# Attention beside the direct blocks of an FFN kernel: three engines in source order, five places per tile, one mixing matmul per tile of the next batch

## The chip, the core and the metric

The kernel runs on one core of one Trainium2 chip. The metric is the time of one execution on the device, in microseconds (us). A core has TensorE (PE; its weight loads are shown apart as PEld), VectorE (DVE), ScalarE (ACT), GpSimd (POOL) and SyncE (SP), which issues nearly all transfers here. Each engine works off a queue of its own in order and waits on semaphores. TensorE's clock is granted at one of two levels, 1.2 or 2.4 GHz; the profile gives the granted clock as a share of the higher one.

## The reference, cut to what matters

Three stages: attention against pooled keys and values, a mixer over tokens with a feed-forward network (FFN), and a Fourier mixer with a normalised FFN.

```python
# 1. B, H, S, D = 8, 8, 576, 64; keys and values are means over 8 positions
k_p = k.reshape(B, H, 72, 8, D).mean(axis=3); v_p = v.reshape(B, H, 72, 8, D).mean(axis=3)
scores = q @ k_p.T / 8; scores -= scores.max(-1)
attn = exp(scores); x = attn / (attn.sum(-1) + 1e-9) @ v_p          # -> (B, S, 512)
# 2. token mixing of rank 32, then FFN 512 -> 2048 -> 512
u = x + ((x.transpose(0, 2, 1) @ U) @ V).transpose(0, 2, 1)
x1 = u + np.maximum(u @ w_ch1, 0) @ w_ch2
# 3. 2D Fourier transform, real part, layer norm, FFN 512 -> 2048 -> 512
u2 = x1 + np.real(fft(fft(x1, axis=1), axis=2)); un = layernorm(u2)
out = u2 + np.maximum(un @ w2_ch1, 0) @ w2_ch2
```

## The kernel before

Everything is fp32 accuracy on TensorE: a matrix is split into a high half (fp32r) and the rest, and a product is three matmuls. `split` (line 108) is that: a ScalarE copy for the high half and a VectorE subtraction for the low one. The 4608 token rows are worked in blocks. First comes a setup (to some 70 us): batch 0's attention, its mixing, the first columns.

**Direct blocks** are the stage that the change is about (some 70 to 862 us): six groups `gi` of 512 rows, and in each group 16 *slots* `f`, one for each 128 hidden columns. A slot has a first product `st1` (line 972: twelve matmuls into bank h0, then `hh` by ScalarE on line 988 and `hl` by VectorE on line 989) and, one slot late, a second product `st2` in two halves (line 995: twelve matmuls in all into four banks of sums). At a group's end the sums are added to their rows and stored (`finish`, line 1015).

Beside that run *lanes*, Python generators, of which the loop on lines 1179 to 1228 takes a step at a time; a yield ends a step, and what a step emits stands in the source between the matmuls of the slot. A slot has two *places* (i = 0, 1), one for each half of `st2`:

- `a` (lines 1054 to 1065), the attention of batches 1 to 7, five tiles of 128 rows each. In `tile_steps` (line 460) a tile takes three steps: scores into banks s0 and s1, with the maximum on VectorE and eight exponentials on ScalarE; the turn of the exponentials through s0 and s1 with two ScalarE copies; the products with V into s0, the scaling on VectorE, the split (`xh`, `xl`) and a store to `xd`. The rank-32 matmuls `hu_mm` of a tile (bank hu) come in the next tile's first step. In group 0 the lane takes a step in each place, later in three of four.
- `mix` (lines 1071 to 1076): when a batch's five tiles are done (`mix_split`, line 545), one matmul for each tile in bank s1 and a VectorE add to the row tile loaded back from `xd` (`mix_mm`, line 552), then a store to `ud`. One tile a place, five in consecutive places. When all five are done, `state["u"]`, the number of rows of `ud` that are ready, moves on.
- `prep`: the pooling of the next batch's keys and values on VectorE; `w`: conversion of weights from 64-bit words (`w_first` for the direct blocks; from group 1 on `w_combine` and `w_second` for the later stages); `p`: the next group's rows loaded, turned (`turn`, VectorE) and split (`settle`) into columns `utx`; `d`: the Fourier stage, once all lanes but `p` are done (`spectral`).

`until` (line 1098) steps lanes without block matmuls until a condition holds. It stands at two points: `p` is started once the next group's rows are in `ud`, from slot 11 on (slot 15 in group 0) by waiting for them; and after slot 15 `until` runs `p` to its end, outside the last group by stepping all lanes. The last splits of the next group's columns follow it.

What sets the order: a planner orders each engine's instructions by its own estimate of times. `manual_schedule` keeps the source's order for the engines that it names: ScalarE from group 1 on (line 1181), and TensorE and VectorE too in the last stage (`chain`, line 1269). `later` and `clock` delay a store to the next slot's start in the source. After 862 us comes the **Strassen stage**: the remaining direct rows and all of the second FFN with seven instead of eight products, with the Fourier lane beside it.

Of the kernel before, what the change touches and what calls it, by code (L numbers as in the profile page):

```python
# [8 lines left out]
F32 = mybir.dt.float32  # L9
F32R = mybir.dt.float32r  # L10
# [11 lines left out]
NPAIR = H // 2  # L22
# [20 lines left out]
NU = 5  # L43
F64_BIAS = float.fromhex("0x1p-112")
# [3 lines left out]
def kernel(  # L48
# [282 lines left out]
    class Attn:  # L331
        def __init__(self, c):
# [12 lines left out]
            self.mixing = False  # L345
            self.done = {}
            self.xq = [scratch(12 + t) for t in range(5)]
# [187 lines left out]
        def tiles(self, b):  # L535
            prev = None
            for t in range(5):
                yield from self.tile_steps(b, t, 0, prev)
                prev = (lambda t=t, x=self.done.pop(t): self.hu_mm(b, t, *x))
            prev()  # L540
            while self.mixing:
                yield
            self.mix_split(b)

        def mix_split(self, b):
            self.mixing = True
# [5 lines left out]
        def mix_mm(self, b, t, x):  # L552
# [5 lines left out]
            if t == 4:  # L558
                self.mixing = False

        def mix(self, b):
            xl = {}

            def load(t):
                n = TT[t][1]
                xl[t] = self.xtile(b)
                nc.sync.dma_start(out=xl[t][:n], in_=xd[b][t])
            load(0)
            yield
            load(1)  # L570
            yield
            for t in range(5):
                self.mix_mm(b, t, xl.pop(t))
                yield
                if t + 2 < 5:
                    load(t + 2)
# [247 lines left out]
    def pair_prep(js):  # L824
        yield from turn(js[0])
        for t in range(NT):
            settle(js[0], t)
            yield
        yield from turn(js[1])
# [185 lines left out]
    def finish(js):  # L1015
        for t in range(4):
# [37 lines left out]
    def lane_a(at):  # L1054
        for b in range(1, B):
# [3 lines left out]
            yield  # L1059
# [9 lines left out]
    mixq = []  # L1069

    def lane_mix(at):
        for b in range(1, B):
            while not mixq:
                yield
            yield from at.mix(mixq.pop(0))
            state["u"] = (b + 1) * S
# [21 lines left out]
    def until(cond, names=None):  # L1098
        n = 0
        state["tick"] = 0  # L1100
        while not cond():
# [4 lines left out]
            assert n < 500, (state, list(lanes))  # L1106

# [33 lines left out]
    lanes["mix"] = lane_mix(at)  # L1141
# [291 lines left out]
```

## Time and profile before

| | us |
|---|---|
| three runs | 1968.53, 1973.78, 1976.72 |
| median | 1973.78 |
| the profiled execution | 1970.54 |
| its span, first to last instruction | 1968.7 |
| TensorE busy in the span | 1846.7 (94%) |
| TensorE weight loads busy | 1596.0 (81%) |
| VectorE, ScalarE, GpSimd busy | 1020.5, 703.7, 196.1 |
| mean granted clock of TensorE | 0.977 |

A busy time is the union of an engine's instructions. Matmuls are pipelined and their ends are modelled, so a busy TensorE is not TensorE at its peak. A wait names the engine and the tile that was waited for, with the line of the instruction that made it. Lines 103, 106 and 113 are helpers (`sub`, `add`, `mm`), so an instruction is told by its tile's name: `utx` the columns of a block, `wo`, `cv` and `wr` weights, `x` rows, `s`, `h`, `o`, `m`, `hu` the banks of PSUM.

### The profile page before, as it was taken

The page shows a single profiled execution, that of the slowest core. Times are in us where ns is not written, and L with a number is a line of the kernel's source. Part 1 is how long each engine was busy: PE and PEld are TensorE (multiplying, and loading weights), DVE is VectorE, ACT ScalarE, POOL GpSimd, SP SyncE. Part 2 cuts the span into 40 slices and gives each one's busy share as a digit, 9 for nine tenths or more (in the row PEclk, how much of TensorE's full clock was granted, in tenths as well). Part 3 has the DMA queues.
Part 4 walks back from the last instruction along what each step waited for, and adds up shares of the span by engine and source line. Part 5 has one row for each costly group of instructions (what it writes and reads, how often), then busy time and mean ns, then how long its engine had stood idle before and what let it go on. Part 6 is the DMA issues. An engine that isn't in the chain of part 4 may idle for free.

```text
span 1968.7 us, 29395 instructions
## 1 busy us (share of the span) xinstructions
PE 1846.7 (94%) x10424; PEld 1596.0 (81%) x10424; DVE 1020.5 (52%) x2265; ACT 703.7 (36%) x2072; POOL 196.1 (10%) x341
## 2 busy tenths in 40 slices
PE   5787689898989999999999999999999999999999
PEld 4676578687767787889899989899989999999998
DVE  7763455555564544444455665656565434444332
ACT  7752434343434341323332433333333323232321
POOL 3430022112121000000000000000000000000000
PEclk9898889899999999999999999999999999999999
DMA  9743463756564646165758786858586766757564
GB/s 360 248 143 112 123 195 133 206 166 206 176 199 152 185 135 202 32 230 196 260 183 287 234 284 194 264 193 263 186 267 192 232 192 210 230 181 234 182 214 129
DMA packets 265779, 394.26 MB, mean 200 GB/s; under 512 B 61664, under 2 KB 92480, under 8 KB 265632
## 3 DMA queue, kind: packets, MB, share of 16 engines
q1 hardware_dynamic: 264704, 388.97, 62.1%
q0 software_dynamic: 928, 3.40, 0.5%
q8 instruction: 83, 1.36, 0.3%
q14 instruction: 64, 0.52, 0.1%
HBM read 312.73 MB, written 79.56 MB: 199 GB/s over the span
## 4 chain that ended last, share of the span: by engine, by line
PE 62%; DMA 3%; DVE 2%; ACT 1%; issue 0%; SPq 0%; DVEq 0%; ACTq 0%
PE h L113 28%; PE o L113 15%; PE m L113 7%; PE hu L113 7%; PE s L113 4%; PE s L901 1%; DMA wr<-wc 1%; DMA x<-x 0%; DMA ul<-ud 0%; DMA ud<-x 0%; DMA x1d<-ur 0%; DMA R<-x1d 0%; DVE hl L1254 0%; DVE xl L103 0%; DVE side L106 0%
## 5 line engine op out<-in xcount | busy, mean ns | idle before, releaser
L113 PEld LDWEIGHTS h<-x,wr 128*128 128x128 f32 x4032 | 527.4, 191 | 31.2 <-DVE side L106 2.5
L113 PE MATMUL h<-x,wr 128*128 128x256 f32 x4032 | 547.6, 283 | 5.2 <-DMA wr<-wc 2.3
L113 PE MATMUL o<-w,hh 128*128 128x512 f32 x1152 | 324.5, 404 | 11.4 <-ACT hh L988 11.2
L113 PE MATMUL h<-utx,w 128*128 128x512 f32 (+1 forms) x1164 | 288.5, 397 | 12.5 <-DVE utx L103 5.7
L113 PEld LDWEIGHTS h<-utx,w 128*128 128x128 f32 x1164 | 219.5, 192 | 62.3 <-DVE utx L103 6.9
L113 PEld LDWEIGHTS o<-w,hh 128*128 128x128 f32 x1152 | 202.8, 192 | 50.0 <-ACT hh L988 21.3
L106 DVE TENSOR_TENSOR side<-h,side 128x256 f32<-128x256 f32 x192 | 106.1, 553 | 145.7 <-PE h L113 144.9
L113 PE MATMUL o<-w,hl 128*128 128x512 f32 x576 | 179.3, 391 | 0.0
L113 PE MATMUL m<-w,hh 128*128 128x512 f32 x576 | 165.5, 395 | 0.2 <-DVE ur L106 0.2
L1248 ACT ACTIVATE hh<-side 128x256 fp32r<-128x256 f32 x192 | 100.0, 521 | 118.5 <-DVE side L106 118.5
L1248 ACT ACTIVATE hh<-h 128x256 fp32r<-128x256 f32 x96 | 36.9, 384 | 278.3 <-PE h L113 275.9
L113 PEld LDWEIGHTS o<-w,hl 128*128 128x128 f32 x576 | 107.9, 188 | 23.6
L1254 DVE SCALAR_TENSOR_TENSOR hl<-h,hh 128x256 fp32r<-128x256 f32 x96 | 40.6, 423 | 157.5 <-ACT hh L1248 157.3
L1254 DVE SCALAR_TENSOR_TENSOR hl<-side,hh 128x256 fp32r<-128x256 f32 x192 | 105.7, 550 | 24.7 <-ACT hh L1248 24.7
L988 ACT ACTIVATE hh<-h 128x512 fp32r<-128x512 f32 x96 | 56.9, 593 | 170.5 <-PE h L113 170.3
L113 PEld LDWEIGHTS m<-w,hh 128*128 128x128 f32 x576 | 103.1, 191 | 17.7 <-DVE ur L106 0.7
L989 DVE SCALAR_TENSOR_TENSOR hl<-h,hh 128x512 fp32r<-128x512 f32 x96 | 65.8, 685 | 87.6 <-ACT hh L988 87.2
L488 ACT ACTIVATE s<-s,mx 128x72 f32<-128x72 f32 x296 | 91.3, 333 | 47.8 <-DVE mx L485 46.0
L113 PE MATMUL hu<-w,hh 128*128 128x512 f32 x384 | 104.7, 394 | 0.0
L113 PE MATMUL m<-w,hl 128*128 128x512 f32 x288 | 97.6, 393 | 0.0
L103 POOL TENSOR_TENSOR wo<-wo 128x256 fp32r<-128x256 f32 x88 | 69.5, 809 | 280.4 <-ACT wo L109 250.5
L103 DVE TENSOR_TENSOR x<-ul,x 128x256 fp32r<-128x256 f32 x154 | 59.2, 420 | 39.6 <-ACT x L109 39.4
(239 smaller groups left out, 2445.0 us busy)
## 6 DMA issues: line engine op xcount, KB each, us to landing
wr<-wc SPq DMA_DIRECT2D x336, 512.0 KB
wc<-wo SPq DMA_DIRECT2D x88, 256.0 KB
x<-x SPq DMA_DIRECT2D x56, 256.0 KB
ur<-ud SPq DMA_DIRECT2D x36, 256.0 KB
x1d<-ur SPq DMA_DIRECT2D x36, 256.0 KB
ul<-u2d SPq DMA_DIRECT2D x36, 256.0 KB
ur<-u2d SPq DMA_DIRECT2D x36, 256.0 KB
out<-ur SPq DMA_DIRECT2D x36, 256.0 KB
```

The source lines that it names most:

```text
L103: eng.tensor_tensor(out=o, in0=a, in1=b, op=ALU.subtract)
L106: eng.tensor_tensor(out=o, in0=a, in1=b, op=ALU.add)
L113: nc.tensor.matmul(o, a, b, start=start, stop=stop, skip_group_check=True)
L488: nc.scalar.activation(out=s[:n, a], in_=v[:, k], func=ACTF.Exp, bias=mx[:n, a:a + 1], accum_out=sm[:n, a:a + 1])
L901: nc.tensor.transpose(o[:, k * 128:k * 128 + 128], u[:, k * 128:k * 128 + 128], ident)
L988: nc.scalar.activation(out=hh, in_=o, func=ACTF.Relu)
L989: nc.vector.scalar_tensor_tensor(out=hl, in0=o, scalar=0.0, in1=hh.bitcast(F32), op0=ALU.max, op1=ALU.subtract)
L1248: nc.scalar.activation(out=hh[:, i], in_=c, func=ACTF.Relu)
L1254: nc.vector.scalar_tensor_tensor(out=hl[:, i], in0=c, scalar=0.0, in1=hh[:, i].bitcast(F32), op0=ALU.max, op1=ALU.subtract)
```

## The change

- `order` now names TensorE, ScalarE and VectorE, from group 1 to the end of the kernel; `chain` is dropped.
- A slot of the direct blocks has three places; the halves of `st2` stand in the first two. Lane `a` steps in all three, `d` in two, `w` four times a slot, `prep` once, `p` three times. In group 0 and once `a` has ended there are further steps of `w`, `prep` and `p`.
- A tile of attention takes five places: scores (and the `hu` matmuls of the tile before), nothing, the turn, the products with V, nothing. `tile_steps` stays for batch 0.
- Lane `mix` is dropped. From batch 3 on, the step with the products with V also mixes the same tile of the batch before, and then loads its next tile. Batches 1 and 7 are mixed by themselves behind their tiles, a tile every second place. `state["u"]` moves with every mixed tile.
- `pair_prep` starts in slot 1 of every group and waits by itself for the rows of each of its blocks. The points of `until` are slot 14 (rows) and slot 15 (end of `p`, stepping `p` alone), both ahead of `st1`; in the last group slot 9. The last splits and the loads of `finish` follow `st1` of slot 15 at once.
- `finish` adds two sums behind each half of the last `st2`.

```diff
+        def kq(self, b, t):
+            q = self.q.pop((b, t))
+            sc = bank("s0"), bank("s1")
+            for p in range(NPAIR):
+                mm(sc[p // 2][:, (p % 2) * 144:(p % 2) * 144 + 144], q[:, p], self.k[:, p], p % 2 == 0, True)
+            self.q_load(5 * b + t + QAHEAD)
...
+            for i in range(2):
+                v = sc[i][:, 0:288].rearrange("p (h k) -> p h k", h=4)
+                nc.vector.tensor_reduce(out=mx[:, 4 * i:4 * i + 4], in_=v, op=ALU.max, axis=AX.X, negate=True)
+                for k in range(4):
+                    a = 4 * i + k
+                    nc.scalar.activation(out=s[:, a], in_=v[:, k], func=ACTF.Exp, bias=mx[:, a:a + 1], accum_out=sm[:, a:a + 1])
...
+        def exp_turn(self):
+            e0, e1 = bank("s0"), bank("s1")
+            for c in range(4):
+                nc.tensor.transpose(e0[:, c * 128:c * 128 + 128], self.s[:, c * 128:c * 128 + 128], ident)
+            nc.tensor.transpose(e1[:, 0:128], self.s[:, 512:640], ident)
...
+            nc.scalar.activation(out=e[:, 0:512], in_=e0, func=ACTF.Copy)
+            nc.scalar.activation(out=e[:, 512:640], in_=e1[:, 0:128], func=ACTF.Copy)
...
+        def av(self, b, t):
+            o = bank("s0")
...
+            xf = self.xtile(b)
+            nc.vector.tensor_tensor(out=xf.rearrange("p (h d) -> p h d", h=H), in0=o.rearrange("p (h d) -> p h d", h=H),
+                                    in1=self.cur.unsqueeze(2).to_broadcast([128, H, D]), op=ALU.mult)
...
+            split(xh, xl, xf)
+            store(xd[b][t], xf[:TT[t][1]])
+            self.done[t] = xh, xl
...
+        def mix_load(self, b, t):
+            n = TT[t][1]
+            self.xm[t] = self.xtile(b)
+            nc.sync.dma_start(out=self.xm[t][:n], in_=xd[b][t])
+
+        def mix_one(self, b, t):
+            self.mix_mm(b, t, self.xm.pop(t))
+            later(lambda: state.update(u=b * S + TT[t][0] + TT[t][1]))
...
     def pair_prep(js):
-        yield from turn(js[0])
-        for t in range(NT):
-            settle(js[0], t)
-            yield
-        yield from turn(js[1])
+        for j in js:
+            while state["u"] < (j + 1) * T:
+                yield
+            yield from turn(j)
+            if j == js[0]:
+                for t in range(NT):
+                    settle(j, t)
+                    yield
...
             at.kv_k(b)
-            yield
             at.kv_v(b)
             started.add(b)
             yield
-            yield from at.tiles(b)
-            mixq.append(b)
-            yield
+            beside = b > 2
+            if beside:
+                at.mix_load(b - 1, 0)
+            for t in range(5):
+                at.kq(b, t)
+                if t:
+                    at.hu_mm(b, t - 1, *at.done.pop(t - 1))
+                yield
+                yield
+                at.exp_turn()
+                yield
+                at.av(b, t)
+                if beside:
+                    at.mix_one(b - 1, t)
+                    if t < 4:
+                        at.mix_load(b - 1, t + 1)
+                yield
+                yield
+            at.hu_mm(b, 4, *at.done.pop(4))
+            at.mix_split(b)
+            yield
+            if b in (1, B - 1):
...
         if gi == 1:
-            order.enter_context(tc.manual_schedule(engines={mybir.EngineType.Activation}))
+            order.enter_context(tc.manual_schedule(engines={mybir.EngineType.PE, mybir.EngineType.Activation, mybir.EngineType.DVE}))
...
+            if last:
+                if f == 9:
+                    until(lambda: state["u"] >= (SB + 1) * TA)
+                if f == 6:
+                    lanes["p"] = prep_a(0)
+            else:
+                if f == 1:
+                    lanes["p"] = pair_prep(groups[gi + 1])
+                if f == NF - 2:
+                    until(lambda: state["u"] >= (gi + 2) * TA)
+                if f == NF - 1:
+                    until(lambda: "p" not in lanes, ["p"])
             hs = st1(js, f, gi == f == 0)
...
+            if f == NF - 1:
+                if not last:
+                    for t in range(NT):
+                        settle(groups[gi + 1][1], t)
+                for t in range(4):
+                    rest(js, t)
...
-            for i in range(2):
-                slot += 1
-                if gi == 0 or slot % 4:
-                    step("a")
-                step("d")
-                if prev:
+            for i in range(3):
+                step("a")
+                if i != 1:
+                    step("d")
+                if prev and i < 2:
                     st2(prev[1], prev[2], i)
-                for name in ("p", "mix", "w", "prep", "w") if f % 4 else ("p", "mix", "w", "prep"):
+                    if prev[1] == NF - 1:
+                        finish(prev[0], (2 * i, 2 * i + 1))
+                for name in (("w", "p"), ("prep", "w", "p"), ("w", "p", "w", "prep"))[i]:
                     step(name)
-                if last:
+                if last or gi == 0:
                     step("p")
-                    step("p")
+                if "a" not in lanes:
+                    step("w")
+                if gi == 0:
+                    step("prep")
+                    step("w")
```

## Rows read from the trace of the kernel before

**Rows 1.** The page, part 2: TensorE's granted clock in 40 slices, tenths.

```profile
PEclk9898889899999999999999999999999999999999
```

**Rows 2.** Windows by stage: stretch, length, busy time of each engine, clock, DMA.

```profile
181.00:247.00 66.00, 38.64 (x167) 28.17 (x166) 28.46 (x54) 23.88 (x102) 2.22 (x5) 0.78 0.51 138
247.00:372.00 125.00, 111.99 (x501) 89.74 (x500) 71.88 (x149) 45.23 (x169) 27.15 (x37) 0.94 0.58 178
372.00:508.00 136.00, 126.45 (x568) 101.14 (x567) 74.34 (x157) 54.51 (x203) 26.30 (x35) 0.94 0.62 185
508.00:641.00 133.00, 121.89 (x563) 98.26 (x562) 72.09 (x151) 53.88 (x200) 22.64 (x31) 0.96 0.56 176
641.00:759.00 118.00, 112.71 (x530) 91.73 (x530) 63.52 (x150) 43.47 (x149) 2.31 (x5) 1.00 0.51 153
759.00:862.00 103.00, 98.56 (x457) 79.85 (x456) 37.12 (x81) 21.10 (x47) 7.17 (x21) 1.00 0.40 126
862.00:1969.00 1107.00, 1095.14 (x6979) 990.81 (x6977) 555.76 (x1325) 353.84 (x885) 48.98 (x140) 1.00 0.68 220
```

**Rows 3.** TensorE's waits from 181 to 247: us in total, times, longest.

```profile
PE s L113 <- DVE x L106: 11.0, 5, 4.1
PE s L492 <- ACT s L488: 6.3, 4, 2.9
```

**Rows 4.** Windows of the six clusters in groups 1 to 3.

```profile
253.00:285.00 32.00, 25.65 (x112) 20.54 (x111) 21.96 (x44) 8.35 (x32) 5.32 (x7) 0.92 0.84 235
357.00:376.00 19.00, 13.34 (x44) 9.36 (x44) 12.97 (x25) 6.42 (x25) 0.00 (x0) 0.72 0.87 259
470.00:486.00 16.00, 12.98 (x50) 10.22 (x50) 8.53 (x17) 5.41 (x24) 2.15 (x3) 0.79 0.67 221
498.00:511.00 13.00, 9.81 (x35) 7.07 (x35) 9.66 (x22) 6.53 (x26) 1.79 (x2) 0.87 0.80 240
558.00:587.00 29.00, 23.83 (x99) 18.57 (x98) 18.04 (x38) 10.36 (x46) 3.61 (x5) 0.88 0.72 233
630.00:646.00 16.00, 12.14 (x49) 8.80 (x48) 9.46 (x23) 7.25 (x27) 0.00 (x0) 0.89 0.73 209
```

**Rows 5.** TensorE's waits from 320 to 870, for the next group's columns.

```profile
PE h L113 <- DVE utx L103: 5.7, 3, 2.5
...
PE h L113 <- ACT utx L109: 3.0, 3, 1.1
```

**Rows 6.** In order of time, 410 to 426: start, us, engine, line, operation, [idle before].

```profile
410.25 2.88 PE L113 MATMUL h<-utx,w 128*128 128x512 f32 x12
...
412.97 0.61 PE L113 MATMUL o<-w,hl 128*128 128x512 f32 x2
...
414.79 0.71 PE L113 MATMUL s<-k,q 128*128 128x144 f32 x4
...
417.53 0.32 ACT L488 ACTIVATE s<-s,mx 128x72 f32<-128x72 f32 x1 [0.70 <-DVE mx L485]
...
419.62 0.35 ACT L488 ACTIVATE s<-s,mx 128x72 f32<-128x72 f32 x1
...
425.11 2.88 PE L113 MATMUL h<-utx,w 128*128 128x512 f32 x12
```

**Rows 7.** Groups of instructions, 150 to 870: busy us, mean ns | idle before.

```profile
L103 POOL TENSOR_TENSOR wo<-wo 128x256 fp32r<-128x256 f32 x88 | 69.5, 809 | 280.4 <-ACT wo L109 250.5 <-DVE wo L103 14.0 <-DVE sm L498 8.5
...
L989 DVE SCALAR_TENSOR_TENSOR hl<-h,hh 128x512 fp32r<-128x512 f32 x85 | 58.2, 685 | 73.3 <-ACT hh L988 72.9
...
L152 DVE SCALAR_TENSOR_TENSOR wo<-cv,wo 128x256 int32<-128x256 int32 x32 | 16.0, 500 | 1.0
...
L152 DVE SCALAR_TENSOR_TENSOR cv<-wo,cv 128x256 int32<-128x256 int32 x32 | 13.3, 422 | 0.7
```

**Rows 8.** VectorE's waits from 320 to 870, for transfers.

```profile
DVE ul L809 <- DMA ul<-ud: 16.5, 10, 5.1
DVE cv L147 <- DMA wd<-cv: 14.5, 11, 2.0
```

More of the change, by code (lines that the diff above doesn't have):

```diff
@@ L43 @@
 NU = 5
+DEBUG = False
 F64_BIAS = float.fromhex("0x1p-112")
@@ L344, in __init__ @@
             self.raw = {}
-            self.mixing = False
             self.done = {}
+            self.xm = {}
             self.xq = [scratch(12 + t) for t in range(5)]
@@ L533, in first @@
                 yield
[L535 to L541, printed above, removed]
-                yield
-            self.mix_split(b)
+        def kq(self, b, t):
[4 more added lines that the diff above has]
+            self.q_load(5 * b + t + QAHEAD)
+            p1 = self.p
+            mx = p1.tile([128, H], F32, tag="mx", name="mx", bufs=2)
+            sm = p1.tile([128, H], F32, tag="sm", name="sm", bufs=2)
+            s = self.s[:, 0:S].rearrange("p (h k) -> p h k", h=H)
+            for i in range(2):
[4 more added lines that the diff above has]
+                    nc.scalar.activation(out=s[:, a], in_=v[:, k], func=ACTF.Exp, bias=mx[:, a:a + 1], accum_out=sm[:, a:a + 1])
+            self.cur = sm
@@ new lines, in exp_turn @@
+        def exp_turn(self):
[3 more added lines that the diff above has]
+            nc.tensor.transpose(e1[:, 0:128], self.s[:, 512:640], ident)
+            e = self.e = self.p.tile([128, 640], F32, tag="e", name="e")
+            nc.scalar.activation(out=e[:, 0:512], in_=e0, func=ACTF.Copy)
+            nc.scalar.activation(out=e[:, 512:640], in_=e1[:, 0:128], func=ACTF.Copy)
+            nc.vector.tensor_scalar(out=self.cur, in0=self.cur, scalar1=1e-9, scalar2=None, op0=ALU.add)
+            nc.vector.reciprocal(out=self.cur, in_=self.cur)
@@ L1013, in rest, with finish @@
         nc.sync.dma_start(out=res[t], in_=ud[r0:r0 + 128, :])
-    def finish(js):
-        for t in range(4):
+    def finish(js, ts=range(4)):
+        for t in ts:
             r = res.pop(t)
@@ L1058, in lane_a @@
             at.kv_k(b)
-            yield
             at.kv_v(b)
@@ L1062, in lane_a @@
             yield
-            yield from at.tiles(b)
-            mixq.append(b)
-            yield
+            beside = b > 2
[18 more added lines that the diff above has]
+            at.mix_split(b)
+            yield
+            if b in (1, B - 1):
+                at.mix_load(b, 0)
+                at.mix_load(b, 1)
+                yield
+                for t in range(5):
+                    yield
+                    at.mix_one(b, t)
+                    yield
+                    if t + 2 < 5:
+                        at.mix_load(b, t + 2)
     ready = set()
     started = {0}
[L1069 to L1076, printed above, removed]
     def lane_prep(at):
@@ L1106, in until @@
             assert n < 500, (state, list(lanes))
+        if n and DEBUG:
+            print("until", n, names, state["slot"], state["u"], list(lanes))
     lanes = {}
@@ L1191 @@
                 ring_load(f - NOP)
-            if not begun and f >= (6 if last else 2):
-                rows = (SB + 1) * TA if last else (gi + 2) * TA
-                ok = lambda: state["u"] >= rows
-                if f >= (NF - 1 if gi == 0 else 11):
-                    until(ok)
-                if ok():
-                    begun = True
-                    lanes["p"] = prep_a(0) if last else pair_prep(groups[gi + 1])
+            if f == NF - 1:
[4 more added lines that the diff above has]
+                    rest(js, t)
             if not df:
@@ L1267 @@
     prev, rows, low = None, None, None
-    chain = ExitStack()
-    chain.enter_context(tc.manual_schedule(engines={mybir.EngineType.PE, mybir.EngineType.DVE}))
     for k in range(len(seq)):
@@ L1327 @@
         st2_a(prev, t)
-    chain.close()
     order.close()
```

31 lines of the change are left out of this document (5 added, 26 removed).

## The prediction

> **What bounds the kernel now.** I read the page first, then the windows by stage, then TensorE's waits inside the bad windows, then one undisturbed stretch in order of time. In the page's forty slices the granted clock of TensorE is full almost everywhere; its dips lie in the first third [rows 1]. The windows tell why. From 862 us on (the Strassen stage) TensorE is busy 1095.14 of 1107 us at clock 1.00, so nothing is to be had there. The direct stage before it is not full. I put the loss of a window as its idle time plus (1 - clock) x length. From 181 to 247 that is 27.4 + 0.22 x 66 = 41.9 us; then 20.5, 17.7 and 16.4 us in the next three windows, 5.3 and 4.4 us in the last two: 106 us in 681 [rows 2]. This stage is bound by TensorE where TensorE has work at hand, and by the latency of the attention chain where it has not.
>
> The 106 us lie in few places.
> - The burst, 181 to 247. Counting places in the source, the last slot of group 0 runs `until` for 16 rounds: the mixing of batch 1 and nearly all attention of batch 2 are emitted with hardly a block matmul between them. TensorE then waits 11.0 us for the VectorE adds of the mixing (five times, all through bank s1), and for ScalarE's exponentials [rows 3]; the clock falls to 1.2 GHz after such idle stretches. 41.9 us.
> - Six clusters in groups 1 to 3, two a group. One is the mixing of five tiles in consecutive places, beside tiles of the next batch that want the same two banks (253, 470, 558 us); the other is the group's end, where the next group's last columns are split after the last block matmul at hand (357, 498, 630 us). By the same formula: 8.9, 11.0, 6.4, 4.9, 8.7 and 5.6 us, 45.5 us in all [rows 4]. At group ends TensorE waits 5.7 us for the VectorE half of the split and 3.0 us for the ScalarE half [rows 5].
> - The rest, 106 - 41.9 - 45.5 = 19 us, is spread over 681 - 66 - 125 = 490 us, about 4%.
>
> **The change part by part.** *Places.* A slot goes from two places to three, and the attention lane takes a step in each (before, three of four from group 1 on). A tile takes five places instead of three. Counted by hand, batch 1 ends its mixing in slot 13 of group 0 instead of behind slot 15, batch 2 starts in slot 14, and no `until` has to run the attention: what is left is two rounds of the p lane at the end of group 0 and none at the later ends. So the burst goes. Its tiles still cost TensorE their matmuls, now beside block matmuls.
>
> *What a place hides.* Twelve block matmuls take 412.97 - 410.25 = 2.72 us; a slot has 24, so 5.44 us, and half of the second product 1.36 us. Two slots with one tile take 425.11 - 410.25 = 14.86 us, which leaves 14.86 - 10.88 = 4.0 us per tile, small waits in it [rows 6]. Three places a slot at five a tile are 0.6 tiles a slot: 5.44 + 0.6 x 4.0 = 7.8 us, against 7.4 now at half a tile. From the scores to the turned exponentials there are two places. In the trace the first score matmul starts at 414.79, the first exponential at 417.53 and the last ends at 419.97: 2.4 us of exponentials, 5.2 us in all, but 417.53 was late because the second half of the scores waited for its bank and VectorE did `hl` in between [rows 6]. With `hl` (0.685 us [rows 7]) done first, I put the chain at some 4.5 us from the first score. TensorE has two halves and the `hu` matmuls there in one phase of three (about 0.9 + 0.5 + 2.7 = 4.1 us), and the first product and one half in the other two (5.5 us). So one tile in three waits about 0.4 to 0.5 us: 31 tiles / 3 x 0.5 = 5 us. From the turn to the products with V there is at least a half, 1.36 us, against two copies of ScalarE; from those to the next scores two places again. I take nothing for these; if VectorE or ScalarE is behind, they cost the same microsecond or so per tile (see the rival).
>
> *Mixing.* One matmul per tile of the next batch replaces five in a row. Its add stands behind the tile's own three VectorE operations, and nobody wants bank s1 for two places. Added waits: that add waits for its load, which is issued only when a tile of the two-buffer ring `xr` is free again, so after the store of the mixed tile before. Queued behind it on VectorE, now in source order, are `hl` of the next slot (which frees bank h0 for the first product after) and the next maximum. A store and a load one after the other have five places, about 13 us. I take 0; the bound is the third rival. Each load and store also passes SP's queue, which no order binds; the number of transfers is unchanged.
>
> *Group ends.* The split of the last columns is emitted before the last halves of the second product, not after them. It needs the end of the first product, `hh`, two ScalarE and two VectorE passes, some 3 us, with 2.7 us of matmuls and the places beside it. I leave 1.5 us for each of five ends, 7.5 us, of the clusters' 45.5.
>
> *Source order on TensorE and VectorE.* From group 1 on the planner no longer moves instructions. The Strassen stage, with all three engines in source order already, shows what that costs when the source is well spaced: 1107 - 1095.14 = 11.9 us, 1.1% [rows 2]. The direct stage has 4% outside the clusters now. From both sides: at 1.1% the rest of 19 us would shrink to about 6; at twice its 4% it would be 40. I keep 4%, the same stage's own value, and charge it to the work that comes out of the burst and the clusters too: (66 - 42) + (125 - 45.5) = 104 us at 4%, 4 us.
>
> *Group 0* stays the planner's. Weight conversion gets up to seven steps a slot, so its ScalarE work is emitted ahead of attention. I charge 4 us, with 0 and 15 as ends: no row shows that order. The spectral lane starts in slot 8 of group 4 instead of slot 1 of group 5; its matmuls come out of the Strassen stage, where TensorE is full, so that moves work and pays nothing; if the cover were not full it would gain 1 to 2 us.
>
> The sum, against the profiled execution's own 1970.54 us: 41.9 + 45.5 - 7.5 - 4 - 5 - 4 = 67 us, less 2 for rounding up idle time that overlaps the low clock: 65. 1970.5 - 65 = 1905.5, say 1906. The profiled execution lies 3.2 us under the median of 1973.78, so this is 3.4% under the median.
>
> **The rivals.** *Slower: VectorE in source order sets the pace.* VectorE is busy 28.5 + 71.9 + 74.3 + 72.1 + 63.5 = 310 us from 181 to 759 [rows 2]; the same work falls into about 64 slots, 4.8 us each of 7.8. To that come its waits in the queue. The weight lane's second operation waits for a ScalarE pass that now stands behind eight exponentials (2.4 us [rows 6], at 0.6 tiles a slot up to 1.5 us a slot), and there are waits for transfers, such as 16.5 us for the columns to be turned and 14.5 us for a conversion buffer [rows 8], perhaps 1.5 us a slot in all. 4.8 + 1.5 + 1.5 = 7.8: just at the slot, so nothing lost as it stands. Every microsecond more per slot costs 64 us, and from 1.0 us the whole gain is gone. With transfers waited for twice as long (1.5 us more): 1906 + 96 = 2002 us. Against it: half the waits occur while TensorE has over 2 us in hand, and a slower slot gives the transfers more time.
>
> The Trainium skill (SBUF — State Buffer, Who interferes with whom) has a rule that speaks for this rival: a VectorE operation with two SBUF operands and a GpSimd operation that reads SBUF lock each other out for the whole instruction. The rows show some of it: the weight lane's `wo<-cv,wo` takes 500 ns where GpSimd's subtractions run and the same shape `cv<-wo,cv` 422 ns where they don't; GpSimd's own take 809 ns [rows 7]. By the rule at its worst, 88 x 0.81 = 71 us would come on top of VectorE, 1.1 us a slot, and the time would be about 1977; by the rows it is 64 x 0.08 = 5 us in all. I go by the rows, and leave the rival's chance as it is.
>
> *Half the gain: the mixing add waits for its load.* At 1 us for each of 35 tiles, passed on to bank s1 and the scores, 35 us: 1941. For it: transfers to and from the same two buffers; SP waits in order. Against: 13 us of room.
>
> *No change: the order alone replaces the planner's with as many stalls.* The burst goes but each of 31 tiles stalls 2 us: about 1906 + 62 = 1968.
>
> **How the numbers follow.** Forecast 0.66, VectorE-bound 0.16, late load 0.12, no change 0.06. Low end: the rest at 1.1% (13 less), group 0 free (4), tiles and ends without a wait (12), and the 4 for moved work: 1906 - 33 = 1873; with an error of 10 us in reading idle time as loss, 1863. High end: the late load at 1941 and group 0 at its worst (11), with part of the VectorE case: 1965. Within 0.5% is about what a measurement of this kernel can tell from no change, so 1964 to 1984 is "same". Faster 0.77 (the forecast, less a sliver, and the late load), same 0.08, slower 0.15.
>
> **What would show it.** Right: one run of slots 7 to 8 us apart from group 0 into group 1 without a hole at 181 to 247; clock 1.00 from there on; no wait for `utx` over 1 us; mixing matmuls one per tile. VectorE rival: TensorE waiting for `hl` or for VectorE's x, with VectorE idle behind ScalarE or transfers at the same time. Late load: VectorE's mixing add waiting for x<-x. The forecast is wrong if slots in groups 1 to 3 take over 8.8 us, or if group 0 lasts over 15 us longer than now.

## The result and the profile after

The changed kernel takes 1883.04 us (median of four runs, 1882.54 to 1883.73) against 1972.97 us for the kernel before (four runs): a ratio of 0.9545, 95% interval 0.9525 to 0.9566, so 89.9 us. The profiled execution took 1883.03 us with a span of 1881.3 us; against the profiled execution before (1970.54) that is 87.5 us less. The forecast was 1906, 65 us less. The sign, the stage and most mechanisms were right; two terms of the sum were wrong in opposite directions.

The page of after, parts 1 and 2: busy time, share and instruction count of each engine, then TensorE's busy tenths and its granted clock in 40 slices of 47 us.

```profile
PE 1811.7 (96%) x10424; PEld 1584.6 (84%) x10424; DVE 1017.3 (54%) x2265; ACT 707.2 (38%) x2072; POOL 194.7 (10%) x341
...
PE   5798899999999999999999999999999999999999
...
PEclk8899799999999999999999999999999999999999
```

The first two slices are the setup (8 and 8 tenths, before 9 and 8). Behind them before had dips over the first third [rows 1]; one is left, in the fifth slice. TensorE runs as many instructions as before, yet its busy time fell from 1846.7 to 1811.7 us; this comes up again below.

Windows of after by stage, in the columns of [rows 2].

```profile
70.00:176.00 106.00, 101.47 (x482) 83.26 (x480) 61.14 (x100) 56.49 (x159) 30.59 (x27) 1.00 0.46 143
176.00:208.00 32.00, 14.46 (x36) 9.55 (x37) 11.82 (x20) 6.31 (x22) 0.00 (x0) 0.57 0.61 153
208.00:324.00 116.00, 115.73 (x591) 97.85 (x590) 75.79 (x169) 58.89 (x230) 30.10 (x42) 1.00 0.59 186
324.00:450.00 126.00, 122.86 (x612) 101.97 (x611) 88.09 (x188) 65.89 (x250) 29.58 (x42) 1.00 0.77 241
450.00:578.00 128.00, 125.44 (x623) 104.67 (x622) 84.65 (x188) 65.14 (x242) 19.69 (x30) 0.99 0.72 221
775.00:1881.30 1106.30, 1098.45 (x6994) 994.21 (x6992) 548.62 (x1306) 350.37 (x879) 46.79 (x135) 1.00 0.71 220
```

The first product of the Strassen stage (the two lines below, before and after: start, us, line, operation) starts 80.9 us earlier, so that much of the gain lies ahead of it.

```profile
862.11 0.87 PE L113 MATMUL h<-x,wr 128*128 128x256 f32 x6
781.19 0.88 PE L114 MATMUL h<-x,wr 128*128 128x256 f32 x6
```

The window from 775 still holds the last second products of the direct blocks. In the Strassen stage itself TensorE stands idle 7.9 us instead of 11.9. By the prediction's formula (idle plus (1 - clock) x length) the hole from 176 to 208 loses 17.5 + 0.43 x 32 = 31.3 us. Groups 1 to 3, where [rows 2] lost 20.5, 17.7 and 16.4 us, lose 0.3, 3.1 and 2.6 + 1.3.

The starts of `hh` give the time from one group's first slot to the next group's, gaps between groups included:

| | before | after | gain |
|---|---|---|---|
| start of group 1 | 213.8 | 208.2 | 5.6 |
| group 1 | 160.7 | 122.9 | 37.8 |
| group 2 | 134.9 | 126.0 | 8.9 |
| group 3 | 133.7 | 127.6 | 6.1 |
| group 4 | 117.7 | 97.8 | 19.9 |
| group 5, to the Strassen stage | 101.3 | 98.7 | 2.6 |

The boundary of groups 0 and 1, of which 41.9 us were forecast, gave its share mainly behind the first slot of group 1, where before emitted batch 2's attention (slots 0 and 1 stood 31.4 us apart, now 8.4). In groups 1 to 3 of after, 15 slots take 114.4, 117.7 and 119.0 us, 7.6 to 7.9 a slot; 7.8 were forecast. The gain in group 4 is attention that is through earlier at that pace: the last scores stand at 599.8 us instead of 727.1.

TensorE's waits of after, in the hole (176 to 208) and from 208 to 775: us in total, times, longest.

```profile
PE s L114 <- DVE x L107: 12.9, 5, 6.2
```

```profile
PE s L114 <- ACT e L560: 2.9, 4, 1.6
PE s L557 <- ACT s L551: 2.4, 7, 1.0
PE s L114 <- ACT k L423: 0.8, 4, 0.3
```

In the hole the wait of [rows 3], for the mixing's VectorE adds through bank s1, is there again, and as long. Behind it no wait is over 1.6 us, and none is for `utx`, for which [rows 5] had 5.7 and 3.0 us.

### The profile page after: what moved, and what is told of

It reads as the page before. It is cut to its first block, busy times and chain, and to the rows that moved or that the text cites. A ratio compares the mean times of both kernels' runs of the same rounds, so it can differ in the third digit from the quotient of the medians.

```text
span 1881.3 us, 29486 instructions
## 1 busy us (share of the span) xinstructions
PE 1811.7 (96%) x10424; PEld 1584.6 (84%) x10424; DVE 1017.3 (54%) x2265; ACT 707.2 (38%) x2072; POOL 194.7 (10%) x341
## 3 DMA queue, kind: packets, MB, share of 16 engines
q1 hardware_dynamic: 264704, 388.97, 66.5%
## 4 chain that ended last, share of the span: by engine, by line
PE 68%; DVE 2%; ACT 1%; DMA 1%; issue 0%; ACTq 0%; SPq 0%; DVEq 0%
PE h L114 31%; PE o L114 16%; PE m L114 8%; PE hu L114 7%; PE s L114 4%; PE s L927 1%; DMA wr<-wc 0%; DMA wd<-cv 0%; DMA x<-x 0%; DVE hl L1307 0%; DVE side L107 0%; ACT hh L1301 0%; PE s L557 0%; ACT s L551 0%; DVE hl L1015 0%
## 5 line engine op out<-in xcount | busy, mean ns | idle before, releaser
L114 PE MATMUL o<-w,hh 128*128 128x512 f32 x1152 | 328.8, 396 | 3.2 <-ACT hh L1014 3.2
L114 PE MATMUL o<-w,hl 128*128 128x512 f32 x576 | 192.3, 392 | 0.0
L1307 DVE SCALAR_TENSOR_TENSOR hl<-side,hh 128x256 fp32r<-128x256 f32 x192 | 105.9, 551 | 29.4 <-ACT hh L1301 28.6
L114 PEld LDWEIGHTS m<-w,hh 128*128 128x128 f32 x576 | 102.2, 189 | 16.5
L551 ACT ACTIVATE s<-s,mx 128x72 f32<-128x72 f32 x280 | 85.6, 329 | 44.8 <-DVE mx L548 44.4
```

The source lines that it names most:

```text
L114: nc.tensor.matmul(o, a, b, start=start, stop=stop, skip_group_check=True)
L551: nc.scalar.activation(out=s[:, a], in_=v[:, k], func=ACTF.Exp, bias=mx[:, a:a + 1], accum_out=sm[:, a:a + 1])
L1307: nc.vector.scalar_tensor_tensor(out=hl[:, i], in0=c, scalar=0.0, in1=hh[:, i].bitcast(F32), op0=ALU.max, op1=ALU.subtract)
```

## The experiments

Ratios are to the kernel before on the same chip; differences to after are taken between medians. Line numbers of after are one or two lower where a kernel adds lines. In the diffs PE, ACT and DVE stand for the engines' long names.

**The two halves of the change.** *Places without the order*: the changed source, but TensorE and VectorE stay with the planner until the last stage.

```diff
-            order.enter_context(tc.manual_schedule(engines={PE, ACT, DVE}))
+            order.enter_context(tc.manual_schedule(engines={ACT}))
...
+    chain.enter_context(tc.manual_schedule(engines={PE, DVE}))
```

> The changed kernel's places, mixing and group ends, but in the direct blocks only ScalarE keeps the source's order, as in the kernel before; TensorE and VectorE are the planner's again there (the last stage keeps all three). If the source order on TensorE and VectorE is what pays, the waits inside groups 1 to 3 come back and the time is 1930 to 1970 us. If the places, the mixing per tile and the group ends pay by themselves, it is 1885 to 1905 us.

Measured 1949.94 us, ratio 0.9877 [0.9849, 0.9905]: 23.5 us of the gain, and so only 1.2%. TensorE's waits from 208 to 850:

```profile
PE o L114 <- ACT hh L1014: 15.2, 18, 1.8
PE s L557 <- ACT s L551: 14.2, 21, 3.5
PE s L114 <- ACT e L560: 6.9, 12, 0.6
```

In the planner's order TensorE comes to second products before their `hh` is there, and to the turn before the exponentials are done; in after the first isn't among the waits listed, and the second is 2.4 us.

*The order without the places*: the kernel before, with all three engines in source order from group 1.

```diff
-            order.enter_context(tc.manual_schedule(engines={ACT}))
+            order.enter_context(tc.manual_schedule(engines={PE, ACT, DVE}))
```

> The kernel before with its two places per slot and its mixing lane, and one edit: TensorE, ScalarE and VectorE in source order from group 1 on. If the order pays by itself: the spread loss of groups 1 to 5 goes while the burst, the mixing in consecutive places and the group ends stay, 1935 to 1955 us. If the places pay: a tile's three steps stand too close together for the source order, TensorE waits for the exponentials at every tile, and the time is 1975 to 2010 us.

Measured 1931.16 us, ratio 0.9778 [0.9759, 0.9797]: 42.3 us. Its waits from 170 to 850 are the kernel before's, by name:

```profile
PE s L113 <- DVE x L106: 12.9, 6, 4.4
PE s L113 <- ACT s L488: 9.9, 5, 2.0
PE h L113 <- ACT utx L109: 8.5, 4, 2.8
```

The burst and the group ends stay. Alone the halves bring 23.5 and 42.3 us, together 89.9: some 24 us exist only when both are there. My reading is that order keeps the spacing that the places provide, and that without spacing it keeps the clusters.

**Group ends.** The last columns are split behind the last halves, as before; all else as after.

```diff
             if f == NF - 1:
-                if not last:
-                    for t in range(NT):
-                        settle(groups[gi + 1][1], t)
...
             hq.append((js, f, hs))
+            if f == NF - 1 and not last:
+                for t in range(NT):
+                    settle(groups[gi + 1][1], t)
```

> The changed kernel with one step of it undone: the splits of the next group's last columns stand behind the last halves of the second product again, as in the kernel before. By the prediction's working an end costs about 3 us of waiting for the two halves of the split, and some low clock: five ends, 1895 to 1908 us. If the ends came out well only because the rows now arrive earlier, 1883 to 1887 us.

Measured 1907.46 us, ratio 0.9658 [0.9628, 0.9689]: 24.4 us over after. Windows over the ends of groups 1 to 3, first this kernel, then after (columns of [rows 2]).

```profile
320.00:345.00 25.00, 20.86 (x89) 16.53 (x88) 13.93 (x27) 11.20 (x38) 7.06 (x12) 0.86 0.66 205
460.00:480.00 20.00, 15.78 (x66) 12.47 (x67) 12.50 (x25) 8.59 (x32) 4.38 (x6) 0.83 0.69 224
590.00:612.00 22.00, 17.73 (x78) 14.30 (x77) 11.57 (x25) 9.14 (x39) 0.00 (x0) 0.84 0.64 187
```

```profile
320.00:345.00 25.00, 24.54 (x120) 20.06 (x119) 17.91 (x37) 12.45 (x40) 7.97 (x12) 1.00 0.76 242
445.00:465.00 20.00, 19.73 (x100) 16.32 (x99) 16.64 (x34) 12.89 (x52) 5.31 (x8) 1.00 0.89 278
570.00:592.00 22.00, 21.55 (x111) 18.04 (x110) 16.10 (x37) 11.71 (x48) 0.00 (x0) 1.00 0.75 218
```

The formula gives 7.6, 7.6 and 7.8 us with the late split and under half a microsecond with the early one. That is some 1.5 us an end too much: from the `hh` of slot 15 to the next group's first, these three ends take 5.9, 5.8 and 5.8 us longer than in after. The formula counts an idle microsecond at the low clock as one and a half. The end of group 4 adds 3.7 us; the four make 21 of the 24.4 us.

**Mixing.** *Behind the own tiles*: every batch is mixed after its tiles, a tile every second place, none beside the next batch.

```diff
-            beside = b > 2
+            beside = False
...
-            if b in (1, B - 1):
+            if True:
```

> The changed kernel with every batch mixed as batches 1 and 7 are: five tiles behind the batch's own five tiles, one every second place, nothing beside the next batch's tiles. If mixing beside the tiles is what removes the mixing clusters (24 us in groups 1 to 3 of the kernel before), they come back in part: 1895 to 1910 us. If it is the spacing, a place between two mixed tiles, and the source order that remove them, 1880 to 1890 us; attention then ends some 17 slots later, which costs nothing while it stays inside the direct blocks.

Measured 1889.95 us, ratio 0.9586 [0.9558, 0.9614], 7 us over after. So it is the spacing of the five matmuls, with the source order (not told apart here), that removes the mixing clusters of [rows 4]; that they stand beside the next batch's tiles adds little.

*A late load*: the row tile is loaded one place ahead of its add instead of five.

```diff
             if beside:
-                at.mix_load(b - 1, 0)
+                pass
...
                 yield
+                if beside:
+                    at.mix_load(b - 1, t)
                 at.exp_turn()
...
-                    if t < 4:
-                        at.mix_load(b - 1, t + 1)
```

> The changed kernel with the mixing's row tile loaded in the place of the tile's own turn, one place ahead of its use instead of five. The prediction's third rival has VectorE's mixing add wait for that load with the slot's other work behind it. If a late load costs what that rival says (1 us a tile and more, 25 tiles), 1905 to 1940 us; if VectorE's idle time and the two free places of bank s1 take it up, 1883 to 1893 us.

Measured 1880.30 us, ratio 0.9533 [0.9514, 0.9552], not told apart from after. Among VectorE's waits from 208 to 578 none of note is for the mixing's rows. The rival of the late load is false for groups 1 to 3.

**VectorE's room.** These two kernels add three reductions that compute nothing used, 0.82 us each, to every slot of groups 1 to 5. First right behind `hl`, so between a tile's scores and their maximum:

```diff
             hs = st1(js, f, gi == f == 0)
+            if gi:
+                for _ in range(3):
+                    nc.vector.tensor_reduce(out=spare, in_=ident.unsqueeze(1).to_broadcast([128, 5, 128]), op=ALU.add, axis=AX.X)
```

> The changed kernel with three useless VectorE reductions (640 elements each, 0.75 us by the pooling's own of 576) behind every first product of groups 1 to 5: 80 x 2.2 = 180 us more VectorE work in source order, nothing left out. If VectorE nearly sets the pace, as the prediction's slower rival has it, most of that lands on the slots: 1960 to 2060 us. If VectorE has the room that the windows show (450 to 578 us: 84.65 busy of 128, 5.1 us of a slot of 7.7), the slots with attention fill up to about 7.3 us and little is lost: 1885 to 1910 us.

Measured 2015.39 us, ratio 1.0222 [1.0193, 1.0252]: 132 us over after. Groups of VectorE instructions, 208 to 900 (busy us, mean ns | idle before), and TensorE's waits there:

```profile
L1251 DVE TENSOR_REDUCE spare<-ident 128x5 f32<-128x640 f32 x234 | 191.4, 818 | 5.4
L1016 DVE SCALAR_TENSOR_TENSOR hl<-h,hh 128x512 fp32r<-128x512 f32 x78 | 53.8, 690 | 102.9 <-ACT hh L1015 102.2
```

```profile
PE s L558 <- ACT s L552: 37.9, 37, 5.4
PE s L115 <- ACT e L561: 16.5, 9, 3.5
```

Then the same load at the end of the slot, behind the third place:

```diff
                     step("w")
+            if gi:
+                for _ in range(3):
+                    nc.vector.tensor_reduce(out=spare, in_=ident.unsqueeze(1).to_broadcast([128, 5, 128]), op=ALU.add, axis=AX.X)
```

> The same three useless reductions per slot as in the run that took 2015 us, but emitted at the slot's end, behind the last place's operations and ahead of the next slot's low half, not between that half and the maximum of the scores. There TensorE waited for the exponentials while VectorE stood idle 102 us ahead of the low halves. If it is latency in the chain from scores to turn that cost 132 us, the load now falls into that idle time: 1885 to 1925 us. If it is VectorE's sum (5.1 + 2.5 us in slots of 7.7), it costs the same wherever it stands: 1990 to 2030 us.

Measured 1951.41 us, ratio 0.9893 [0.9873, 0.9913]: 68 us over after, between the two ranges, so neither cause is the whole. Groups 1 to 3, by the starts of `hh`:

| us per slot | group 1 | group 2 | group 3 |
|---|---|---|---|
| after | 7.6 | 7.8 | 7.9 |
| load behind `hl` | 9.7 | 10.1 | 10.1 |
| load at the slot's end | 8.4 | 8.9 | 8.9 |

The first costs 2.1 to 2.3 of its 2.45 us a slot, though VectorE still stands idle for 102 us until `hh` comes: TensorE waits for exponentials (37.9 us) that started late. The second costs 0.8 to 1.1 us a slot. The load is the same in both, so the 64 us between them are the latency that it adds where it delays a tile's maximum; at the slot's end, where less waits for it, some 1.4 us a slot of VectorE's time are free. In the last six slots of group 4, which hold no attention, the load costs nothing in either place (5.4 us a slot in all three kernels).

**The hole at 176 us.** It lies where group 0 ends, and there the planner still orders. *Source order from group 0*:

```diff
-        if gi == 1:
+        if gi == 0:
             order.enter_context(tc.manual_schedule(engines={PE, ACT, DVE}))
```

> The changed kernel with the source order from group 0 instead of group 1. The hole from 176 to 208 us (17.5 us idle and 13.8 us at the low clock) is the mixing of batch 1, which the planner put behind everything else of group 0. If the planner's order is its cause, the mixing moves up, the hole goes and the time is 1850 to 1862 us. If the cause is data (batch 1's tiles are late because weight conversion fills ScalarE and VectorE until 133 us, and group 1's columns need the mixed rows), the hole stays or is spread over group 0, and the time is 1878 to 1900 us.

Measured 1913.45 us, ratio 0.9689 [0.9661, 0.9717]: 30 us over after. TensorE's waits from 60 to 230:

```profile
PE s L114 <- ACT k L423: 21.8, 1, 21.8
PE s L114 <- ACT e L560: 14.9, 2, 11.5
```

That is over both ranges. The first three slots take 21 to 25 us each: the attention stands behind weight conversion in the queues. *The same with fewer conversion steps in a slot of group 0*:

```diff
-                for name in (("w", "p"), ("prep", "w", "p"), ("w", "p", "w", "prep"))[i]:
+                for name in (("w", "p"), ("prep", "w", "p"), ("w", "p", "w", "prep"))[i] if gi else (("w", "p"), ("prep", "p"), ("w", "p", "prep"))[i]:
...
                     step("prep")
-                    step("w")
```

> The changed kernel with all three engines in source order from group 0 and weight conversion at three steps a slot there instead of seven. With seven, TensorE waited 21.8 us for batch 1's keys behind conversion on ScalarE. If the pile of conversion in slots 0 to 3 is the cause of that wait, it goes, and the hole of the planner's order with it: 1850 to 1872 us. If one and a half conversions a slot still fill ScalarE (some 7 us of it a slot), slots 0 to 8 take 9 to 10 us each: 1880 to 1900 us.

Measured 1888.81 us, ratio 0.9573 [0.9557, 0.9589]. The edit leaves two of the loop's seven steps, not three. The wait for the keys falls from 21.8 to 2.8 us, so conversion was the cause of that wait, but slots 1 to 9 now take 7 to 19 us and 6 us over after remain. A gap is left at the end of group 0 too: slots 13 and 14 stand 16.8 us apart. There TensorE's fifth mixing matmul waits for VectorE's fourth mixing add. VectorE, held to the source's order, has the pooling of the next batch ahead of that add, and each pooling step waits for its transfer: 9.0 us for keys and 8.0 for values from 160 to 215. (The pooling has five steps a slot in group 0 and two later, not one as the description of the change has it.) One row of TensorE, one of VectorE:

```profile
187.66 0.79 PE L114 MATMUL s<-hst,vst 128*128 128x512 f32 x1 [8.04 <-DVE x L107]
...
178.59 0.69 DVE L416 TENSOR_REDUCE vp<-raw 128x64 f32<-128x512 f32 x1 [2.26 <-DMA raw<-vr]
```

*Order from slot 8 of group 0*:

```diff
+            if gi == 0 and f == 8:
+                order.enter_context(tc.manual_schedule(engines={PE, ACT, DVE}))
```

> The changed kernel with the source order from slot 8 of group 0. With the order from slot 0 TensorE waited 21.8 us for batch 1's keys, behind weight conversion; by slot 8 the conversion is emitted. If what costs there is only the conversion's place in the queues, the mixing now stands between block matmuls and the hole goes: 1850 to 1865 us. If batch 1's tiles, emitted before slot 8 and still the planner's, are late all the same, the ordered part waits for them and the hole only moves: 1880 to 1900 us.

Measured 1890.32 us, ratio 0.9588 [0.9537, 0.9639], 7 us over after. Mixing moves up from 178-187 to 164-185, but between slots 8 and 9 a gap of 22.6 us opens (128.4 to 151). Most of the hole has moved to the seam between planner and source order; the gap between slots 13 and 14 is there as well (15.3 us).

*Attention ahead in the planner*: its steps in group 0 are marked urgent.

```diff
-                step("a")
+                if gi == 0:
+                    with urgent():
+                        step("a")
+                else:
+                    step("a")
```

> The changed kernel with batch 1's attention and mixing, and the start of batch 2, marked urgent for the planner in group 0, as the setup's attention is. If the hole from 176 to 208 us comes from the planner putting attention behind weight conversion and block products, the tiles move up (a tile every 18 us now) and the hole shrinks: 1855 to 1875 us. If the tiles are late because ScalarE, VectorE and GpSimd are busy with the conversion until 133 us, the conversion is late instead and block products wait: 1885 to 1905 us.

Measured 1883.71 us, ratio 0.9555 [0.9527, 0.9582], no change. Tiles of batch 1 start at 78, 100, 114, 135 and 154 us, nearly as in after (83, 98, 114, 135, 155). Neither theory had that; the planner's marks do not reach what delays these tiles.

*TensorE alone in source order in group 0*, ScalarE and VectorE from group 1:

```diff
-        if gi == 1:
-            order.enter_context(tc.manual_schedule(engines={PE, ACT, DVE}))
+        if gi < 2:
+            order.enter_context(tc.manual_schedule(engines=({PE}, {ACT, DVE})[gi]))
```

> The changed kernel with TensorE alone in source order in group 0; ScalarE and VectorE stay the planner's there, all three are ordered from group 1 on. In the planner's group 0 the eight exponentials of a tile are cut in two by the next slot's high half, and scores, turn and products with V stand a slot apart, 18 us a tile where the ordered groups take 12.6. If the planner, given TensorE's order, fits the other two engines to it, the tiles end earlier and the hole shrinks: 1852 to 1872 us. If conversion keeps ScalarE from following, TensorE waits in place as it did with all three ordered: 1890 to 1915 us.

Measured 1875.24 us (1873.42 to 1877.16), ratio 0.9507 [0.9493, 0.9521]: faster than both kernels, 8 us under after with intervals that don't meet, and between the two ranges. Its windows over the same stretches:

```profile
70.00:176.00 106.00, 91.33 (x424) 73.66 (x423) 67.06 (x102) 56.19 (x160) 28.83 (x27) 0.95 0.51 158
176.00:208.00 32.00, 31.47 (x157) 26.08 (x156) 17.80 (x36) 12.98 (x48) 0.66 (x1) 1.00 0.61 159
```

The hole is gone: 31.47 of 32 us busy at clock 1.00. Block matmuls of group 0 now wait their turn and stand between the mixing matmuls (166.4 to 181.0). But by the formula the stretch ahead loses 14.7 + 5.3 = 20 us where after lost 4.5; slots 2 to 5 start at 81.6, 102.1, 110.2 and 121.8. Group 1 starts at 199.2 instead of 208.2. Part of it can be read. Between slots 2 and 3, 20.5 us apart, TensorE, held to its order, waits three times, 6.2 us in all, for tiles of V, which GpSimd writes between its passes of weight conversion; the first product behind that runs at the low clock:

```profile
88.73 1.01 PE L114 MATMUL s<-v,e 128*128 128x192 f32 x2 [3.36 <-POOL v L429]
...
94.03 4.83 PE L114 MATMUL h<-utx,w 128*128 128x512 f32 x12
```

What delays the slots behind that wasn't settled.

## Why the prediction was right and where not

**The burst: the step that failed.** The prediction let all 41.9 us go, because by the count of places in the source batch 1's mixing ends in slot 13. That count holds where the source sets the order (with TensorE ordered, the five mixing matmuls do stand in slots 11 to 13); in group 0 it does not. The prediction itself wrote that group 0 stays the planner's, and counted there by the source all the same. The planner issued batch 1's tiles some 18 us apart and its mixing at 178 to 187, after the block matmuls of group 0 had run out. TensorE in order of time (start, us, line, operation, [idle before]):

```profile
174.64 0.62 PE L114 MATMUL o<-w,hl 128*128 128x512 f32 x2
...
180.53 0.80 PE L114 MATMUL s<-hst,vst 128*128 128x512 f32 x1 [0.78 <-DVE x L107]
...
187.25 0.80 PE L114 MATMUL s<-hst,vst 128*128 128x512 f32 x1 [1.52 <-DVE x L107]
194.20 1.33 PE L114 MATMUL s<-k,q 128*128 128x144 f32 x4 [6.16 <-DVE x L107]
...
202.87 5.30 PE L114 MATMUL h<-utx,w 128*128 128x512 f32 x12 [1.17 <-ACT utx L110]
```

From 176 to 202.87 there is no block matmul: group 1's first product needs the rows that batch 1's mixing makes, and the twelve matmuls then take 5.30 us instead of 2.9, at the low clock. What did go is the other half of the burst, batch 2's attention emitted without blocks. The burst of before in two windows:

```profile
181.00:208.00 27.00, 10.27 (x30) 6.48 (x29) 11.74 (x20) 5.78 (x22) 0.00 (x0) 0.56 0.65 156
208.00:247.00 39.00, 28.37 (x139) 21.69 (x139) 16.72 (x35) 18.10 (x80) 2.22 (x5) 0.94 0.42 126
```

By the formula the first half lost 28.6 us and is still there with 31.3; the second lost 13.0 and is gone. In time the hole costs less than 31.3: at a mean clock of 0.57, 27.5 of its 32 us lay at the lower level and only 14.46 were busy, so 17.54 + 14.46 / 2 = 24.8 us at most. In the same way at least 23.8 - 10.27 = 13.5 us of idle time in the first row lay at the lower level, so that the formula counts 6.7 us too much there; the prediction took off 2 for all windows together.

The kernel with TensorE in source order has no hole, so the data don't force one at that place. But its group 1 starts only 9.0 us earlier, because slots of group 0 are late instead. How much of the rest is order and how much is attention that is ready late stays open. The prediction's own signs held this test ("without a hole at 181 to 247"), and it failed.

In the hole the late-load rival's mechanism does occur, for batch 1, whose mixing stands by itself. VectorE's waits, 176 to 210:

```profile
DVE x L107 <- DMA x<-x: 5.7, 3, 3.7
```

**Clusters: right.** None of the six of [rows 4] is left. The 7.5 us kept for group ends were too many: TensorE had enough matmuls to cover the split (experiment on group ends). The mixing clusters went by spacing and order.

**The rest, moved work, turn waits and group 0: too dear.** The prediction kept 19 us and added 4, 5 and 4. All of 208 to 775 loses some 8 us: 567 us at 1.4%, near the 1.1% of the Strassen stage, which stood in the prediction as the low bound. Group 0 ahead of the hole takes 104.4 us for 15 slots, 104.3 before: its term is 0.

**A gain that the formula does not see: a term that was missing.** By the formula the loss of the stretch that the prediction looked at fell from 106 to 39.5 us, 66.5. Ahead of it, in group 0, idle time fell by another 2.5 us, from 7.0 (103.99 of 111 us busy from 70 to 181) to 4.5, and in the Strassen stage by some 4: about 73 of the measured 87.5. TensorE's busy time fell by 35.0 us at the same number of instructions, and the low clock can hold at most (0.023 x 1968.7) - (0.014 x 1881.3) = 19 us of that. So at least some 16 us of waits had been drawn as busy time, close to the 14.5 that the formula misses. A tile shows it. The same view, 232 to 244 in after:

```profile
232.92 1.14 PE L114 MATMUL s<-k,q 128*128 128x144 f32 x8
...
234.36 0.63 PE L114 MATMUL h<-w,hh 128*128 128x512 f32 x2
...
238.49 0.60 PE L557 MATMUL s<-ident,s 128*128 128x128 f32 x4
...
238.95 0.71 PE L114 MATMUL o<-w,hh 128*128 128x512 f32 x2
...
240.43 1.53 PE L114 MATMUL s<-v,e 128*128 128x128 f32 x10
...
241.76 0.71 PE L114 MATMUL h<-w,hh 128*128 128x512 f32 x2
```

From start to start a tile costs 1.44 + 0.46 + 1.33 = 3.2 us, where the prediction took 4.0 from a stretch of before [rows 6] and called the small waits in it part of the tile. In that stretch the tile's own matmuls take 3.6 us from start to start, and 0.4 us lie in the block matmuls beside them. Both kinds of matmul hold a part of what is missing: added up over both traces at full clock, from each matmul's start to the next, less idle time and what a matmul of its kind usually takes, attention has some 9 us less in after and the blocks some 6. No run separates this; it is worked out.

The balance by the formula, from 65 to 87.5: -31.3 for the hole, +7.5 group ends, +13 for the three surcharges, +10.4 of the rest, +2 rounding, +6.5 in group 0 and the Strassen stage, +14.5 unseen by the formula, together 22.6. In the prediction's own stretch the sum came close, 65 against 66.5, by errors that cancel: that was luck.

**The rivals.** VectorE setting the pace is real as a mechanism: 2.4 us a slot bring 132 us. The prediction put its room at zero; at the slot's end it is some 1.4 us, and the waits for transfers that were counted against it have mostly gone. Before, the two largest kinds took 16.5 and 14.5 us [rows 8]; in after, from 247 to 760, the second takes 5.8 us and the first has gone from the waits listed there. The argument against the rival, that a slower slot gives transfers more time, can't be the reason, since slots did not get slower; that loads are now asked for at even distances may be, and was only argued. "No change" is answered by the first two experiments: either half alone is faster, by 1.2 and 2.2%.

The rule of the Trainium skill (SBUF — State Buffer, Who interferes with whom), that a VectorE operation with two SBUF operands and a GpSimd operation that reads SBUF lock each other out, against the rows of after, 150 to 780:

```profile
L154 DVE SCALAR_TENSOR_TENSOR wo<-cv,wo 128x256 int32<-128x256 int32 x32 | 15.0, 469 | 5.5 <-ACT cv L149 3.5
L154 DVE SCALAR_TENSOR_TENSOR cv<-wo,cv 128x256 int32<-128x256 int32 x32 | 13.6, 426 | 11.4 <-ACT wo L149 9.0
```

469 ns beside 426, closer together than in [rows 7]. These means mix instructions that meet a GpSimd instruction with others that don't. One by one (after, from 345 us):

```profile
345.02 0.74 POOL L104 TENSOR_TENSOR wo<-wo 128x256 fp32r<-128x256 f32 x1 [10.62 <-DVE wo L104]
345.13 0.92 DVE L153 SCALAR_TENSOR_TENSOR wo<-cv,wo 128x256 int32<-128x256 int32 x1
346.15 0.42 DVE L154 SCALAR_TENSOR_TENSOR wo<-cv,wo 128x256 int32<-128x256 int32 x1
```

The one that starts beside GpSimd's subtraction takes 0.92 us and ends 0.28 us after it; the next, by itself, takes 0.42. Wherever a `wo<-cv,wo` of this stage starts while a GpSimd instruction is running, it ends 0.28 us after it, in both traces. So the traces agree with the rule of the Trainium skill. What was small is the number of meetings: of the 64 `wo<-cv,wo` 18 overlapped a GpSimd instruction before (751 ns in the mean, the others 417) and 11 after (709), some 6 and 3 us in all. The prediction's small total by the rows held, not a lock at every instruction.

## What to carry to other kernels

Source order and spacing belong together: give each lane step a place at a distance of its latency, then hold the engines to that order; each alone brought a quarter to a half of the gain. Emit a block's last split ahead of the last independent matmuls. Before counting places in the source, find out where the region that keeps this order begins; at its border the planner's order counts, and there the largest remaining loss may lie.

## What the runs showed that was not expected

The same VectorE load cost 132 us in one place of the slot and 68 us in another. VectorE's busy share is lower in the dearer kernel, since the same work is spread over more time: the share says little about an engine in the middle of a chain. With the late split each of three group ends stood idle for 4.1 to 4.3 us and cost 5.8 to 5.9: the rest is the lower clock behind the idle time. A wait can hide inside a busy TensorE: of the 35 us of busy time that vanished with the instruction count unchanged, at least 16 were not the clock's. And the mean time of an instruction can hide a lock that its few meetings show plainly.
